# Folding batches 2 to 7 of a Fourier stage with accumulating transfers

## The chip, the cores and the metric

The kernel runs on one core of one Trainium2 chip. The metric is the device time of one execution in microseconds. Each kernel is run several times, and the median is compared. The profile is that of one further execution, with its own time and its own span (from the first to the last instruction).

## The reference

For each of 8 batches of 3072 x 256 numbers the kernel computes the real part of a two-dimensional Fourier transform, and sends every resulting row through a maxout network: three products with w1, w2 and w3, the largest of the three, and a product with w_out.

```python
def _attn_ref(x):                       # x: (8, 3072, 256) float32
    X = np.fft.fft(x, axis=1)
    X = np.fft.fft(X, axis=2)
    return X.real.astype(np.float32)

def _moe_ref(x, w1, w2, w3, w_out):     # x: (24576, 256), w: (256, 768), w_out: (768, 256)
    h = np.maximum(np.maximum(x @ w1, x @ w2), x @ w3)
    return (h @ w_out).astype(np.float32)
```

## The kernel before

All products run in bf16 on TensorE. The Fourier transform over 256 columns is folded into the weights at the start (`gE`, `gO`, `gD`, `gw`). What is left per batch is the transform over 3072 rows, in two stages, and the network.

**Loading and turning.** The 3072 rows of a batch are split as 24 x 128, the 256 columns as 4 groups of 64. A chunk `xs` has 96 partitions (4 column groups x 24 row groups) and 32 of the 128 rows, with 64 columns each; four chunks make a batch. `load_rows` (L107) and `load_next` (L119) issue the loads on SyncE's queue (SP). Pool then converts each chunk to bf16 and changes the order, so that the 128 rows stand next to each other for each column: the natural half (columns 0 to 32 of a group, L155) and a reversed half (rows and columns backwards, L158). This is `turn_chunk`, cut into four parts per chunk, two natural and two reversed. The real part of the transform combines each value with its mirror image, and the kernel does so inside the matmul.

**Stage one.** `Mix.s` takes the turned tile as stationary operand, one column at a time. For each of 33 columns it runs two matmuls into the same place of PSUM: the natural column against `m24f` (L496) and the reversed column against `m24r` (L498). `m24r` names the mirrored partitions. Pieces s0 to s5 hold five columns each, s6 holds three (0, 32 and 1). ScalarE evicts the piece into `z_all` (L503, L506, L507).

**Stage two.** `Mix.k` runs four matmuls or more per piece against the table `tab` (L522, L524) and ScalarE evicts into `t` (L526). Pieces k0 to k5 each make 256 of the 1536 columns of `t`; `end` adds a last one.

**The network.** A batch has 3 blocks of 512 columns, each with 6 units, one per slice of 128 of the hidden width: 18 units. A unit runs four matmuls of 512 columns (L542, L543), an evicting relu on ScalarE (L556) and a maximum on VectorE (L557), and then two matmuls (L550) that turn the same PSUM banks into the values of the mirrored rows. Twelve times per batch a slot opens a bank `po` (two banks in all) with a matmul (L591); VectorE makes `other` from it (L594), Pool adds that to `even` (L597), twelve hidden matmuls collect in the bank (L567), and VectorE adds bank and `even` into `ot` (L617). Half of `ot` is scattered by Pool (L620, followed by a tiny memset, L624), half is stored by SP (L630). There are six `ot` buffers and two banks `ps` for the pieces and `pl` (L580).

**The order.** Each engine executes its instructions in the order in which the program writes them. The last loop of the program goes over batches, blocks and units, and a plan, `at(b, unit, fn)`, says which further work is written after which unit (units above 17 fall into the next batch). While batch b is in the network, the plan holds the pieces of batch b + 1, from unit `begin[b]` on, one a unit, the turning of batch b + 2 and the loads of batch b + 3:

```python
begin = [11, 6] + [5] * (B - 3)
at(b, 6 + 4 * ch + part if b else 11 + 11 * (4 * ch + part) // 16, ... turn_chunk(b + 2, ch, part))
at(b, UNITS + (0, 1, 2, 4 if b else 6)[ch], lambda b=b, ch=ch: fetch(b + 3, ch))
```

Batch 0 is prepared ahead of the loop and batch 1 mostly in its first units, by code of their own.

Of the kernel before, what the change touches and what calls it, by code (L numbers as in the profile page):

```python
# [10 lines left out]
BF16 = mybir.dt.bfloat16  # L11
INT32 = mybir.dt.int32
AX = mybir.ActivationFunctionType
ALU = mybir.AluOpType
# [19 lines left out]
def kernel(  # L34
# [9 lines left out]
    nc = tc.nc  # L44

    B, S, D = x.shape
# [3 lines left out]
    TOKB = 512  # L50
# [9 lines left out]
    consts = ctx.enter_context(tc.tile_pool(name="consts", bufs=1))  # L60
    ps_f = ctx.enter_context(tc.tile_pool(name="ps_f", bufs=2, space=bass.MemoryType.PSUM))
    xs_pool = ctx.enter_context(tc.tile_pool(name="xs", bufs=4))
    x0_pool = ctx.enter_context(tc.tile_pool(name="x0", bufs=2))
    t_pool = ctx.enter_context(tc.tile_pool(name="tbuf", bufs=2))

    m24f = consts.tile([96, 96], BF16, tag="m24f")
# [28 lines left out]
    t_mid = consts.tile([128, 2, B], BF16, tag="t_mid")  # L95
    z_all = consts.tile([128, 128 * 26], BF16, tag="z_all")
    z = z_all.rearrange("p (c r) -> p c r", r=26)

    def x_rows(b):
        return x[b].rearrange("(a bb) (g dl) -> g a bb dl", bb=128, g=4)  # L100
# [31 lines left out]
    raw = {}  # L132
    turned = {}

    def reverse(copy, xr, xs, r0, n, d0=32, d1=65):

        last = r0 + n > 128
        for (lo, hi, m) in ((d0, min(d1, 64), n), (64, d1, n - 1)) if last else ((d0, d1, n),):
            if lo < hi:
                copy(out=xr[:, lo - 32:hi - 32, 129 - r0 - m:129 - r0],  # L140
                     in_=bass.AP(xs.tensor, xs.offset + (m - 1) * 64 + lo,
                                 [xs.ap[0], [1, hi - lo], [-64, m]]))

    def turn_chunk(b, ch, part=None):

        if (b, "v") not in turned:
            x0 = x0_pool.tile([96, 66 * 130], BF16, name="x0", tag="x0")
            v = x0.rearrange("p (dl bb) -> p dl bb", bb=130)
            turned[b] = (lambda d: v[:, d, 0:128], rows_back(v[:, 33:66, :]))
            turned[b, "v"] = v  # L150
        v = turned[b, "v"]
        xs = raw[b, ch]
        for (d0, d1) in (((0, 17), (17, 33))[part % 2:part % 2 + 1] if part is not None else ((0, 33),)):
            if part is None or part < 2:
                nc.gpsimd.tensor_copy(v[:, d0:d1, ch * 32:ch * 32 + 32],  # L155
                                      xs[:, 0:32 * 64].rearrange("p (bb dl) -> p dl bb", dl=64)[:, d0:d1, :])
            if part is None or part >= 2:
                reverse(lambda out, in_: nc.gpsimd.tensor_copy(out, in_), v[:, 33:66, :], xs,  # L158
                        ch * 32, 33 if ch == 3 else 32, 32 + d0, 32 + d1)

    def signed():
        nc.scalar.activation(out=gw[:, 514:770], in_=gw[:, 256:512], func=AX.Copy, scale=sgn)
# [17 lines left out]
    def rows_back(v):  # L180
        return lambda d: v[:, 32 - d, 0:128] if d else v[:, 32, 1:129]
# [17 lines left out]
        nc.gpsimd.iota(t, pattern, base=base, channel_multiplier=cm,  # L199
                       allow_small_or_imprecise_dtypes=True)  # L200

    x0_first = x0_pool.tile([96, 64 * 130], BF16, name="x0", tag="x0")
    x0v = x0_first.rearrange("p (bb dl) -> p bb dl", dl=64)
    xs_a = xs_pool.tile([96, 33 * 64], FP32, name="xs", tag="xs")
    rows_a = xs_a.rearrange("p (bb dl) -> p bb dl", dl=64)
    load_rows((nc.sync, nc.sync, nc.scalar, nc.scalar), rows_a[:, 0:16, :], 0, 112, 128)
# [37 lines left out]
    for (name, value) in (("rnd", ROUND), ("n24", -24.0)):  # L244
        c = gen.tile([128, 1], FP32, name=name, tag=name)
# [17 lines left out]
    turn = 2.0 * math.pi  # L263
# [34 lines left out]
    for (r0, r1) in ((0, 3), (3, 7)):  # L298
# [5 lines left out]
                          in_=up[:, 0:13].unsqueeze(1).to_broadcast([96, 2, 13]))  # L304
# [36 lines left out]
    for (m, c, by) in ((m24f, 0, ind24), (m24r, 24, ind24[:, ::-1])):  # L341
        nc.vector.tensor_tensor(
            out=m.rearrange("p (g r) -> p g r", g=4),
            in0=t24[:, c:c + 24].unsqueeze(1).to_broadcast([96, 4, 24]),
            in1=by.unsqueeze(2).to_broadcast([96, 4, 24]), op=ALU.mult)
    for (m, c, own) in ((m0f, 0, 1), (m0r, 24, 3)):
# [7 lines left out]
        out=dvec.rearrange("p (dl g) -> p dl g", g=4),  # L354
# [55 lines left out]
    for ch in range(4):  # L410
# [11 lines left out]
                        in_=moe_w_out.rearrange("(jc p) c -> p jc c", jc=NJC))  # L422
# [56 lines left out]
    class Mix:  # L479
# [7 lines left out]
        def s(self, k, x0, pool=ps_f, evict=nc.scalar.copy):  # L487

            ps1 = pool.tile([128, 512], FP32, name="ps1", tag="ps")
            if k < len(DLS):  # L490
                parts = [(d, 96, m24f, m24r) for d in range(*DLS[k])]
            else:
                parts = [(0, 52, m0f, m0r), (32, 48, m24f, m24r), (1, 96, m24f, m24r)]
            c0 = 0
            for (d, n, mf, mr) in parts:
                nc.tensor.matmul(ps1[:, c0:c0 + n], x0[0](d), mf[:, 0:n],  # L496
                                 start=True, stop=False)
                nc.tensor.matmul(ps1[:, c0:c0 + n], x0[1](d), mr[:, 0:n],  # L498
                                 start=False, stop=True)
                c0 += n  # L500
            if k < len(DLS):
                lo = 4 * DLS[k][0]
                evict(out=z[:, lo:lo + 20, 0:24],  # L503
                      in_=ps1[:, 0:480].rearrange("p (c r) -> p c r", r=24))
            else:
                evict(out=z_all[:, 0:52], in_=ps1[:, 0:52])  # L506
                evict(out=z[:, 2:8, 0:24],  # L507
                      in_=ps1[:, 52:196].rearrange("p (c r) -> p c r", r=24))
# [42 lines left out]
                             skip_group_check=True)  # L551

    def unit_out(pses, dst, n):
        stmp = h_pool.tile([128, TOKB], BF16, name="stmp", tag="stmp")
        src3 = pses[1][:, 0:n]
        nc.scalar.activation(out=stmp[:, 0:n], in_=pses[0][:, 0:n], func=AX.Relu)  # L556
        nc.vector.tensor_tensor(out=dst, in0=src3, in1=stmp[:, 0:n], op=ALU.max)  # L557
# [6 lines left out]
    def l2_hidden(po, hcols):  # L564
        for jc in range(NJC):
            yield
            nc.tensor.matmul(po, hcols(jc), wout_bf[:, jc * 256:(jc + 1) * 256],  # L567
                             start=False, stop=(jc == NJC - 1), skip_group_check=True)
# [101 lines left out]
    def l2_mid():  # L670

        hmid = h_pool.tile([128, NJC, B], BF16, name="hmid", tag="hmid")
        n = NJC * B
        psm = ps_f.tile([128, 512], FP32, name="psm", tag="ps")
        for i in range(2):
            for jc in range(NJC):
                js = slice(jc * 128, (jc + 1) * 128)
                cs = slice(i * n + jc * B, i * n + (jc + 1) * B)
                nc.tensor.matmul(psm[:, cs], gE[i][:, js], t_mid[:, 0, :],
                                 start=True, stop=False)  # L680
                nc.tensor.matmul(psm[:, cs], gO[i][:, js], t_mid[:, 1, :],
                                 start=False, stop=True)
                yield
        stmp = h_pool.tile([128, TOKB], BF16, name="stmp", tag="stmp")
        nc.scalar.activation(out=stmp[:, 0:n], in_=psm[:, 0:n], func=AX.Relu)
        nc.vector.tensor_tensor(out=hmid.rearrange("p jc n -> p (jc n)"), in0=psm[:, n:2 * n],
                                in1=stmp[:, 0:n], op=ALU.max)
        po = ps_f.tile([128, 512], FP32, name="pom", tag="ps")
        for _ in range(6):
            yield  # L690
        for k in range(2):
            nc.tensor.matmul(po[0:B, 0:256], t_mid[:, k, :], gw[:, k * 256:(k + 1) * 256],
                             start=(k == 0), stop=(k == 1))
            yield
        yield from l2_hidden(po[0:B, 0:256], lambda jc: hmid[:, jc, :])
        ot = out_pool.tile([128, 512], FP32, name="ot", tag="ot")
        nc.vector.tensor_copy(out=ot[0:B, 0:256], in_=po[0:B, 0:256])
        stored(nc.sync.dma_start(out=out[NHALF: NHALF + S * (B - 1) + 1: S, :],
                                 in_=ot[0:B, 0:256]), "direct", ("scattered",))
# [28 lines left out]
    first = prep_first(0, lambda: slots.pop(0).tile([128, 512], FP32, name="psg", tag="ps"))  # L728
# [10 lines left out]
    h_pool = ctx.enter_context(tc.tile_pool(name="hbuf", bufs=2))  # L739
# [23 lines left out]
    def at(b, unit, fn):  # L763
        plan.setdefault((b + unit // UNITS, unit % UNITS), []).append(fn)

    def piece(b, what):
        mm = mix(b)
        if what[0] == "s":
            mm.s(int(what[1:]), turned[b])
        elif what[0] == "k":  # L770
            mm.k(int(what[1]))
        else:
            mm.end()
# [4 lines left out]
    ahead = (("s0",), ("s1",), ("s2",), ("s3",), ("s4",), ("s5",), ("s6",),  # L778
             ("k0",), ("k1",), ("k2",), ("k3",), ("k4",), ("k5", "end"))
    first_ahead = (11, 12, 13, 13, 14, 14, 15, 16, 16, 17, 18, 19, 20)  # L780
    begin = [11, 6] + [5] * (B - 3)

    def l2_first():
        for _ in l2_even(0, 0):
# [17 lines left out]
    for b in range(B - 1):  # L802
        for i, whats in enumerate(ahead):
            for what in whats:
                at(b, begin[b] + i if b else first_ahead[i], lambda b=b, what=what: piece(b + 1, what))
        if b + 2 < B:
            for ch in range(4):
                for part in range(4):
                    at(b, 6 + 4 * ch + part if b else 11 + 11 * (4 * ch + part) // 16,
                       lambda b=b, ch=ch, part=part: turn_chunk(b + 2, ch, part))  # L810
                if b + 3 < B:
                    at(b, UNITS + (0, 1, 2, 4 if b else 6)[ch], lambda b=b, ch=ch: fetch(b + 3, ch))

    for b in range(B):
# [77 lines left out]
```

## Time and profile before

| | us |
|---|---|
| median of 3 runs | 413.03 |
| lowest and highest of them | 412.92, 413.54 |
| the profiled execution | 412.64 |
| its span | 410.9 |
| TensorE busy | 397.4 |
| Pool busy | 320.7 |
| VectorE busy | 308.7 |
| ScalarE busy | 266.5 |

In the profile's rows PE is TensorE's matmuls, PEld its loads of the stationary operand, DVE VectorE, ACT ScalarE, POOL GpSimd and SP SyncE; a q behind the name is that engine's queue of issued instructions. A row names the line of the program, the operation, the tile written and the tiles read, shapes and count. The idle time given with a group is the time that the engine stood still just before its instructions, and the arrow names what ended it. Rows of a timeline begin with start and length in microseconds from the start of the span. The ends of matmuls are modelled, so their starts are the better measure.

### The profile page before, as it was taken

Reading aid. Unit: us, or ns where it says so; the run is one execution under the profiler, and the core shown is the slowest. Engines: PE = TensorE matmul, PEld = TensorE weight load, DVE = VectorE, ACT = ScalarE, POOL = GpSimd, SP = SyncE. Lnnn points to the kernel's source line nnn. Section 1 sums busy time; section 2 is a strip of 40 time slices with the busy share of each in tenths; the row PEclk is TensorE's granted clock in tenths of the full one; section 3 lists DMA queues with packets and bytes.
Section 4 is the critical chain, followed back from the end, with each engine's and each line's share of the span. In section 5 each row is a group of like instructions: output and inputs, shape, how many; then the busy total and the mean of one; then the engine's idle time right before and its main releaser. Section 6 shows DMA issues by size and latency. Waiting matters only on the chain.

```text
span 410.9 us, 9097 instructions
## 1 busy us (share of the span) xinstructions
PE 397.4 (97%) x3072; PEld 269.2 (66%) x3072; DVE 308.7 (75%) x556; ACT 266.5 (65%) x489; POOL 320.7 (78%) x428
## 2 busy tenths in 40 slices
PE   0999999999999999999999999999999999999996
PEld 0465677766676677667666667667666666766665
DVE  8798767776768777786778777787768767778884
ACT  6787766766666667657765766666775676655550
POOL 9599999998888888888789798888878844446651
PEclk9999999999999999999999999999999999999999
DMA  9999885784228841586218942386411121212214
GB/s 116 185 198 183 188 210 143 184 193 104 100 80 210 181 130 53 144 209 139 99 65 191 193 133 86 95 195 144 143 65 70 61 78 64 79 53 53 104 65 142
DMA packets 131111, 52.70 MB, mean 128 GB/s; under 512 B 113009, under 2 KB 128120, under 8 KB 131064
## 3 DMA queue, kind: packets, MB, share of 16 engines
q1 hardware_dynamic: 106496, 37.50, 37.5%
q0 software_dynamic: 23632, 14.29, 16.3%
q8 instruction: 24, 0.39, 0.4%
q10 hardware_dynamic: 936, 0.33, 0.3%
q14 instruction: 23, 0.19, 0.2%
HBM read 29.02 MB, written 25.17 MB: 132 GB/s over the span
## 4 chain that ended last, share of the span: by engine, by line
PE 95%; DVE 2%; ACT 1%; issue 0%; POOL 0%; ACTq 0%; POOLq 0%
PE po L567 30%; PE pse L542 15%; PE pse L550 15%; PE pse L543 15%; PE ps L496 3%; PE ps L498 3%; PE po L591 3%; PE ps L522 3%; PE ps L524 3%; PE pl L580 2%; PE warm L713 2%; DVE hm L557 1%; PE psw L465 0%; DVE w L276 0%; ACT stmp L556 0%
## 5 line engine op out<-in xcount | busy, mean ns | idle before, releaser
L556 ACT ACTIVATE stmp<-pse 128x512 bf16<-128x512 f32 x288 | 171.2, 600 | 44.7 <-PE pse L543 29.7
L557 DVE TENSOR_TENSOR hp<-pse,stmp 128x512 bf16<-128x512 f32 x144 | 99.6, 691 | 87.2 <-ACT stmp L556 60.1
L620 POOL DMA_INDIRECT out_dram<-ot,rows_m x92 | 102.8, 1118 | 53.2 <-DVE ot L617 40.1
L542 PE MATMUL pse<-t,gE 128*128 128x512 bf16 x288 | 109.2, 379 | 0.5
L543 PE MATMUL pse<-t,gO 128*128 128x512 bf16 x288 | 109.0, 378 | 0.0
L557 DVE TENSOR_TENSOR hm<-pse,stmp 128x512 bf16<-128x512 f32 x144 | 99.2, 689 | 3.8 <-ACT stmp L556 3.5
L567 PE MATMUL po<-wout_bf,hp 128*128 128x256 bf16 x576 | 85.9, 272 | 0.0
L550 PE MATMUL pse<-t,gD 128*128 128x512 bf16 x288 | 85.6, 379 | 0.0
L567 PE MATMUL po<-wout_bf,hm 128*128 128x256 bf16 x570 | 85.3, 273 | 0.0
L597 POOL TENSOR_TENSOR even<-even,other 128x256 f32<-128x256 f32 x92 | 66.5, 723 | 22.3 <-DVE other L594 19.8
L567 PEld LDWEIGHTS <-hp 128*128 128x128 bf16 x576 | 56.3, 98 | 17.1 <-issue 1.9
L567 PEld LDWEIGHTS <-hm 128*128 128x128 bf16 x576 | 56.4, 98 | 16.6
L617 DVE TENSOR_TENSOR ot<-po,even 128x512 f32<-128x512 f32 x92 | 62.8, 682 | 0.0
L158 POOL CAST x<-xs 96x544 bf16<-96x544 f32 (+5 forms) x57 | 60.7, 1071 | 0.0
L155 POOL CAST x<-xs 96x544 bf16<-96x544 f32 (+2 forms) x51 | 59.0, 1159 | 0.3 <-DMA xs<-in_x_dram 0.3
L526 ACT CAST t<-ps 128x512 bf16<-128x512 f32 x48 | 27.9, 586 | 34.5 <-PE ps L524 34.4
L550 PEld LDWEIGHTS <-gD 128*128 128x128 bf16 x288 | 27.9, 98 | 32.2
L503 ACT CAST z_all<-ps 128x480 bf16<-128x480 f32 x46 | 25.4, 560 | 33.7 <-PE ps L498 33.7
L594 DVE SCALAR_TENSOR_TENSOR other<-twice,po 128x256 f32<-128x256 f32 x92 | 43.8, 476 | 0.1
L543 PEld LDWEIGHTS <-gO 128*128 128x128 bf16 x288 | 28.1, 98 | 20.3 <-issue 2.0
L542 PEld LDWEIGHTS <-gE 128*128 128x128 bf16 x288 | 28.1, 98 | 19.6 <-issue 0.7
L583 ACT COPY even<-pl 128x512 f32<-128x512 f32 x46 | 27.0, 588 | 10.1 <-PE pl L580 10.1
(171 smaller groups left out, 383.7 us busy)
## 6 DMA issues: line engine op xcount, KB each, us to landing
xs<-in_x_dram SPq DMA_DIRECT2D x84, 198.0 KB
out_dram<-ot SPq DMA_DIRECT2D x90, 128.0 KB
xs<-in_x_dram SPq DMA_DIRECT2D x28, 192.0 KB
raw_w<-in_moe_w_dram SPq DMA_DIRECT2D x4, 384.0 KB
out_dram<-ot,rows_m POOLq DMA_INDIRECT x92, 3.8
out_dram<-ot SPq DMA_DIRECT2D x17, 64.0 KB
x<-in_x_dram POOLq DMA_DIRECT2D x8, 120.0 KB, 6.1
xs<-in_x_dram SPq DMA_DIRECT2D x32, 5.8 KB
```

Source lines behind the costliest of these rows:

```text
L155: nc.gpsimd.tensor_copy(v[:, d0:d1, ch * 32:ch * 32 + 32], xs[:, 0:32 * 64].rearrange("p (bb dl) -> p dl bb", dl=64)[:, d0:d1, :])
L158: reverse(lambda out, in_: nc.gpsimd.tensor_copy(out, in_), v[:, 33:66, :], xs, ch * 32, 33 if ch == 3 else 32, 32 + d0, 32 + d1)
L542: nc.tensor.matmul(pse[:, 0:n], gE[i][:, js], te, start=True, stop=False)
L543: nc.tensor.matmul(pse[:, 0:n], gO[i][:, js], to, start=False, stop=True)
L550: nc.tensor.matmul(pse, gD[i][:, js], to, start=False, stop=True, skip_group_check=True)
L556: nc.scalar.activation(out=stmp[:, 0:n], in_=pses[0][:, 0:n], func=AX.Relu)
L557: nc.vector.tensor_tensor(out=dst, in0=src3, in1=stmp[:, 0:n], op=ALU.max)
L567: nc.tensor.matmul(po, hcols(jc), wout_bf[:, jc * 256:(jc + 1) * 256], start=False, stop=(jc == NJC - 1), skip_group_check=True)
L594: nc.vector.scalar_tensor_tensor(out=other, in0=twice, scalar=po[:, 256:257], in1=po[:, 0:256], op0=ALU.mult, op1=ALU.subtract)
L597: nc.gpsimd.tensor_tensor(out=line[:, 256:512], in0=line[:, 0:256], in1=other, op=ALU.add)
L617: nc.vector.tensor_tensor(out=ot, in0=po, in1=lin, op=ALU.add)
L620: stored(nc.gpsimd.indirect_dma_start(out, bass.IndirectOffsetOnAxis(ap=rows_m[0:128 - lo, b * 12 + slot: b * 12 + slot + 1], axis=0), ot[ ...
```

## The change

For batches 2 to 7 the sum of each value and its mirror image is formed before stage one. Pool writes the natural half into a tile `xw` and the mirrored half, with rows and columns backwards, into one buffer `xb`; column 33 of `xw` takes the few values that have no partner. `send_turned` issues eight stores on SP that bring `xb` to DRAM, 12 partitions each. `add_turned` issues two transfers from Pool that read the stored half back with its partitions in reverse order and add it into `xw` (`accum_op`), 16 columns each. `Mix.s` then runs one matmul per column, against `m24f`, and two for column 0 alone.

The plan moves with it. In batches from 1 on, the parts of the turning stand at units 5 to 18 instead of 6 to 21, in an order that brings the mirrored parts of the last two chunks ahead of their natural parts; the sends stand at unit 16 and the adds at unit 20 (in batch 0 at 20 and 24). The pieces begin at unit 9 in batch 1 and at unit 6 in the later ones, one later than before, and in batch 6 none stands later than unit 17. The pitch of the turned tile goes from 130 to 128, the tile of batches 0 and 1 has one buffer, and `stmp` is 16 columns wider. Batches 0 and 1 keep their two matmuls per column.

```diff
@@ -60,7 +60,9 @@
     consts = ctx.enter_context(tc.tile_pool(name="consts", bufs=1))
     ps_f = ctx.enter_context(tc.tile_pool(name="ps_f", bufs=2, space=bass.MemoryType.PSUM))
     xs_pool = ctx.enter_context(tc.tile_pool(name="xs", bufs=4))
-    x0_pool = ctx.enter_context(tc.tile_pool(name="x0", bufs=2))
+    x0_pool = ctx.enter_context(tc.tile_pool(name="x0", bufs=1))
+    xw_pool = ctx.enter_context(tc.tile_pool(name="xw", bufs=2))
+    turn_pool = ctx.enter_context(tc.tile_pool(name="turn", bufs=2, space=bass.MemoryType.DRAM))
     t_pool = ctx.enter_context(tc.tile_pool(name="tbuf", bufs=2))
 
     m24f = consts.tile([96, 96], BF16, tag="m24f")
@@ -95,6 +97,8 @@
     t_mid = consts.tile([128, 2, B], BF16, tag="t_mid")
     z_all = consts.tile([128, 128 * 26], BF16, tag="z_all")
     z = z_all.rearrange("p (c r) -> p c r", r=26)
+    xb = consts.tile([96, 32 * 128], BF16, tag="xb")
+    mir = xb.rearrange("p (dl bb) -> p dl bb", bb=128)
 
     def x_rows(b):
         return x[b].rearrange("(a bb) (g dl) -> g a bb dl", bb=128, g=4)
@@ -141,22 +145,61 @@
                      in_=bass.AP(xs.tensor, xs.offset + (m - 1) * 64 + lo,
                                  [xs.ap[0], [1, hi - lo], [-64, m]]))
 
-    def turn_chunk(b, ch, part=None):
+    def turn_chunk(b, ch):
 
         if (b, "v") not in turned:
-            x0 = x0_pool.tile([96, 66 * 130], BF16, name="x0", tag="x0")
-            v = x0.rearrange("p (dl bb) -> p dl bb", bb=130)
+            x0 = x0_pool.tile([96, 68 * 128], BF16, name="x0", tag="x0")
+            v = x0[:, 0:66 * 130].rearrange("p (dl bb) -> p dl bb", bb=130)
             turned[b] = (lambda d: v[:, d, 0:128], rows_back(v[:, 33:66, :]))
             turned[b, "v"] = v
         v = turned[b, "v"]
         xs = raw[b, ch]
-        for (d0, d1) in (((0, 17), (17, 33))[part % 2:part % 2 + 1] if part is not None else ((0, 33),)):
-            if part is None or part < 2:
-                nc.gpsimd.tensor_copy(v[:, d0:d1, ch * 32:ch * 32 + 32],
-                                      xs[:, 0:32 * 64].rearrange("p (bb dl) -> p dl bb", dl=64)[:, d0:d1, :])
-            if part is None or part >= 2:
-                reverse(lambda out, in_: nc.gpsimd.tensor_copy(out, in_), v[:, 33:66, :], xs,
-                        ch * 32, 33 if ch == 3 else 32, 32 + d0, 32 + d1)
+        nc.gpsimd.tensor_copy(v[:, 0:33, ch * 32:ch * 32 + 32],
+                              xs[:, 0:32 * 64].rearrange("p (bb dl) -> p dl bb", dl=64)[:, 0:33, :])
+        reverse(lambda out, in_: nc.gpsimd.tensor_copy(out, in_), v[:, 33:66, :], xs,
+                ch * 32, 33 if ch == 3 else 32)
+
+    def turn_part(b, ch, part):
+
+        xs = raw[b, ch]
+        if b not in turned:
+            xw = xw_pool.tile([96, 34 * 128], BF16, name="xw", tag="xw")
+            turned[b] = xw.rearrange("p (dl bb) -> p dl bb", bb=128)
+        v = turned[b]
+        half, natural = part % 2, part // 2
+        if natural:
+            d0, d1 = ((0, 17), (17, 33))[half]
+            nc.gpsimd.tensor_copy(v[:, d0:d1, ch * 32:ch * 32 + 32],
+                                  xs[:, 0:32 * 64].rearrange("p (bb dl) -> p dl bb", dl=64)[:, d0:d1, :])
+            return
+        c0 = 96 - 32 * ch
+        d0, d1 = ((0, 16), (16, 32))[half]
+        nc.gpsimd.tensor_copy(mir[:, d0:d1, c0:c0 + 32],
+                              bass.AP(xs.tensor, xs.offset + 33 * 64 - 1 - d0,
+                                      [xs.ap[0], [-1, d1 - d0], [-64, 32]]))
+        if half:
+            nc.gpsimd.tensor_copy(v[:, 33, c0:c0 + 32],
+                                  bass.AP(xs.tensor, xs.offset + 32 * 64, [xs.ap[0], [-64, 32]]))
+
+    held = {}
+
+    def send_turned(b):
+
+        hd = turn_pool.tile([8, 12 * 4096], BF16, name="held", tag="held")
+        for i in range(8):
+            nc.sync.dma_start(out=hd[7 - i].rearrange("(a r) -> a r", a=12),
+                              in_=xb[i * 12:(i + 1) * 12])
+        held[b] = hd
+
+    def add_turned(b):
+
+        hd = held[b]
+        v = turned[b]
+        for c in range(2):
+            nc.gpsimd.dma_start(out=v[:, 1 + 16 * c:17 + 16 * c, :].rearrange("p dl bb -> p (dl bb)"),
+                                in_=bass.AP(hd.tensor, hd.offset + 11 * 4096 + 2048 * c,
+                                            [[12 * 4096, 8], [-4096, 12], [1, 2048]]),
+                                accum_op=ALU.add)
 
     def signed():
         nc.scalar.activation(out=gw[:, 514:770], in_=gw[:, 256:512], func=AX.Copy, scale=sgn)
@@ -199,8 +242,8 @@
         nc.gpsimd.iota(t, pattern, base=base, channel_multiplier=cm,
                        allow_small_or_imprecise_dtypes=True)
 
-    x0_first = x0_pool.tile([96, 64 * 130], BF16, name="x0", tag="x0")
-    x0v = x0_first.rearrange("p (bb dl) -> p bb dl", dl=64)
+    x0_first = x0_pool.tile([96, 68 * 128], BF16, name="x0", tag="x0")
+    x0v = x0_first[:, 0:64 * 128].rearrange("p (bb dl) -> p bb dl", dl=64)
     xs_a = xs_pool.tile([96, 33 * 64], FP32, name="xs", tag="xs")
     rows_a = xs_a.rearrange("p (bb dl) -> p bb dl", dl=64)
     load_rows((nc.sync, nc.sync, nc.scalar, nc.scalar), rows_a[:, 0:16, :], 0, 112, 128)
@@ -493,10 +536,15 @@
                 parts = [(0, 52, m0f, m0r), (32, 48, m24f, m24r), (1, 96, m24f, m24r)]
             c0 = 0
             for (d, n, mf, mr) in parts:
-                nc.tensor.matmul(ps1[:, c0:c0 + n], x0[0](d), mf[:, 0:n],
-                                 start=True, stop=False)
-                nc.tensor.matmul(ps1[:, c0:c0 + n], x0[1](d), mr[:, 0:n],
-                                 start=False, stop=True)
+                if isinstance(x0, tuple):
+                    pairs = ((x0[0](d), mf), (x0[1](d), mr))
+                elif d:
+                    pairs = ((x0[:, d, :], mf),)
+                else:
+                    pairs = ((x0[:, 0, :], mf), (x0[:, 33, :], mr))
+                for i, (st, mv) in enumerate(pairs):
+                    nc.tensor.matmul(ps1[:, c0:c0 + n], st, mv[:, 0:n], start=(i == 0),
+                                     stop=(i == len(pairs) - 1))
                 c0 += n
             if k < len(DLS):
                 lo = 4 * DLS[k][0]
@@ -551,7 +599,7 @@
                              skip_group_check=True)
 
     def unit_out(pses, dst, n):
-        stmp = h_pool.tile([128, TOKB], BF16, name="stmp", tag="stmp")
+        stmp = h_pool.tile([128, TOKB + 16], BF16, name="stmp", tag="stmp")
         src3 = pses[1][:, 0:n]
         nc.scalar.activation(out=stmp[:, 0:n], in_=pses[0][:, 0:n], func=AX.Relu)
         nc.vector.tensor_tensor(out=dst, in0=src3, in1=stmp[:, 0:n], op=ALU.max)
@@ -681,7 +729,7 @@
                 nc.tensor.matmul(psm[:, cs], gO[i][:, js], t_mid[:, 1, :],
                                  start=False, stop=True)
                 yield
-        stmp = h_pool.tile([128, TOKB], BF16, name="stmp", tag="stmp")
+        stmp = h_pool.tile([128, TOKB + 16], BF16, name="stmp", tag="stmp")
         nc.scalar.activation(out=stmp[:, 0:n], in_=psm[:, 0:n], func=AX.Relu)
         nc.vector.tensor_tensor(out=hmid.rearrange("p jc n -> p (jc n)"), in0=psm[:, n:2 * n],
                                 in1=stmp[:, 0:n], op=ALU.max)
@@ -778,7 +826,9 @@
     ahead = (("s0",), ("s1",), ("s2",), ("s3",), ("s4",), ("s5",), ("s6",),
              ("k0",), ("k1",), ("k2",), ("k3",), ("k4",), ("k5", "end"))
     first_ahead = (11, 12, 13, 13, 14, 14, 15, 16, 16, 17, 18, 19, 20)
-    begin = [11, 6] + [5] * (B - 3)
+    begin = [11, 9] + [6] * (B - 3)
+    turn_order = [(ch, part) for ch, part in zip((0, 0, 0, 0, 1, 1, 1, 1, 2, 2, 3, 3, 2, 2, 3, 3),
+                                                 (0, 1, 2, 3, 0, 1, 2, 3, 0, 1, 0, 1, 2, 3, 2, 3))]
 
     def l2_first():
         for _ in l2_even(0, 0):
@@ -802,13 +852,16 @@
     for b in range(B - 1):
         for i, whats in enumerate(ahead):
             for what in whats:
-                at(b, begin[b] + i if b else first_ahead[i], lambda b=b, what=what: piece(b + 1, what))
+                at(b, min(begin[b] + i, 17 if b == B - 2 else 99) if b else first_ahead[i],
+                   lambda b=b, what=what: piece(b + 1, what))
         if b + 2 < B:
-            for ch in range(4):
-                for part in range(4):
-                    at(b, 6 + 4 * ch + part if b else 11 + 11 * (4 * ch + part) // 16,
-                       lambda b=b, ch=ch, part=part: turn_chunk(b + 2, ch, part))
-                if b + 3 < B:
+            first, width, send_at, add_at = (5, 14, 16, 20) if b else (11, 11, 20, 24)
+            for i, (ch, part) in enumerate(turn_order):
+                at(b, first + width * i // 16, lambda b=b, ch=ch, part=part: turn_part(b + 2, ch, part))
+            at(b, send_at, lambda b=b: send_turned(b + 2))
+            at(b, add_at, lambda b=b: add_turned(b + 2))
+            if b + 3 < B:
+                for ch in range(4):
                     at(b, UNITS + (0, 1, 2, 4 if b else 6)[ch], lambda b=b, ch=ch: fetch(b + 3, ch))
 
     for b in range(B):
```

## The prediction

> **What bounds the kernel now.** I read the page's busy times and granted clock first, then the chain of work that ended last.
>
> ```profile
> PE 397.4 (97%) x3072; PEld 269.2 (66%) x3072; DVE 308.7 (75%) x556; ACT 266.5 (65%) x489; POOL 320.7 (78%) x428
> ...
> PEclk9999999999999999999999999999999999999999
> ...
> PE 95%; DVE 2%; ACT 1%; issue 0%; POOL 0%; ACTq 0%; POOLq 0%
> ```
>
> TensorE is busy for 97% of the span at the full granted clock, and 95% of the chain runs through it. A busy share alone proves little, since the ends of matmuls are modelled; what counts is the pitch at which they start. The timeline of TensorE shows it for one stage-one piece and its neighbours (start, length, line, tile):
>
> ```profile
> 181.18 0.21 PE L496 MATMUL ps<-m24f,x 96*128 96x96 bf16 x1
> 181.22 0.20 PE L498 MATMUL ps<-m24r,x 96*128 96x96 bf16 x1
> ...
> 181.56 0.21 PE L498 MATMUL ps<-m24r,x 96*128 96x96 bf16 x1
> 181.60 0.38 PE L542 MATMUL pse<-t,gE 128*128 128x512 bf16 x1
> ...
> 182.47 0.59 PE L550 MATMUL pse<-t,gD 128*128 128x512 bf16 x2
> 182.90 0.27 PE L591 MATMUL po<-gw,t 128*128 128x257 bf16 x1
> ```
>
> Ten matmuls start within 0.42 us (181.18 to 181.60), 42 ns apart, and the next unit's first matmul starts on the same grid: no wait on either side. The steady rhythm is read from the chain in order of time, where one and the same place comes back each batch:
>
> ```profile
> 168.79 0.98 PE po L567 x9
> ...
> 216.04 0.98 PE po L567 x9
> ...
> 263.40 0.98 PE po L567 x9
> ...
> 310.65 0.98 PE po L567 x9
> ```
>
> A batch takes 47.3 us ((310.65 - 168.79) / 3), a unit (18 per batch) 2.63 us. The next engine is Pool, so I read busy time by stretches (length, then PE, PEld, DVE, ACT, POOL, clock, DMA share, GB/s): one stretch in which the turning of a batch runs, and one late, almost without it.
>
> ```profile
> 204.00:253.00 49.00, 49.00 (x383) 33.66 (x382) 36.41 (x62) 32.16 (x60) 41.60 (x56) 1.00 0.53 135
> ...
> 302.00:351.00 49.00, 49.00 (x387) 34.01 (x386) 37.17 (x63) 31.63 (x59) 32.78 (x47) 1.00 0.20 70
> ```
>
> **The saving on TensorE.** Of the 33 matmul pairs of a batch's stage one (six pieces of 5, one of 3), all but d = 0 become one matmul: 32 go, one of them 48 columns wide. At 42 ns each, the short one at half: 31 x 0.042 + 0.02 = 1.32 us a batch, for batches 2 to 7 7.9 us, all on the engine that sets the end. Nothing is added to TensorE. The batch becomes 46.0 us, the unit 2.55 us.
>
> **Pool.** It issued what the groups of instructions list (count, busy us, mean ns, idle before):
>
> ```profile
> L620 POOL DMA_INDIRECT out_dram<-ot,rows_m x92 | 102.8, 1118 | 53.2 <-DVE ot L617 40.1 <-issue 8.5 <-DMA xs<-in_x_dram 2.3
> L155 POOL CAST x<-xs 96x544 bf16<-96x544 f32 x24 | 27.3, 1137 | 0.0
> L158 POOL CAST x<-xs 96x544 bf16<-96x544 f32 x18 | 20.8, 1155 | 0.0
> L158 POOL CAST x<-xs 96x512 bf16<-96x512 f32 x18 | 19.5, 1086 | 0.0
> L107 POOL DMA_DIRECT2D x<-in_x_dram x12 | 11.8, 1002 | 0.3 <-issue 0.3
> L158 POOL CAST x<-xs 96x561 bf16<-96x561 f32 x6 | 7.0, 1163 | 0.0
> L158 POOL CAST x<-xs 96x495 bf16<-96x495 f32 x6 | 6.3, 1046 | 0.0
> L158 POOL CAST x<-xs 96x32 bf16<-96x32 f32 x6 | 1.4, 228 | 0.0
> ```
>
> The natural casts (L155) stay. The reversed ones cost (20.8 + 19.5 + 7.0 + 6.3 + 1.4) / 6 = 9.2 us a batch; in their place come 8 of 96x512 at 1.086 and 4 of 96x32 at 0.228, 9.6 us: +0.4. Two accumulating DMAs are added. The trace has none; the nearest rows are the plain loads that Pool issues (1.0 us) below and its slowest scatter (2.6 us) above. I take 1.0, since a row of 96 transfers resembles those loads: +2.0. Busy before is 41.6 x 47.3 / 49 = 40.2 us a batch, so 42.6 of 46.0 after, and 44.7 with the 0.17 us (8.5 / 51) of issue gap in front of its 12 scatters: still under TensorE, by 1.3 us. But the 16 casts now fall into 14 units instead of 16, and Pool will run late inside that stretch by 1 to 2 us. Who waits for a late Pool is the final add (L617), through L597:
>
> ```profile
> 182.04 0.72 POOL L597 TENSOR_TENSOR even<-even,other 128x256 f32<-128x256 f32 x1 [0.68 <-DVE other L594]
> ...
> 186.94 0.68 DVE L617 TENSOR_TENSOR ot<-po,even 128x512 f32<-128x512 f32 x1
> ```
>
> The sum ready at 182.76 is used at 186.94: 4.2 us of cover. I price Pool's lag at 0.4 us in all (0 to 3 us); beyond 4.2 us it goes straight to VectorE, then to the two `po` banks and TensorE.
>
> **The new transfers.** One mirrored half is 96 x 4096 x 2 bytes = 0.79 MB. The queue rows and the scatter's landing time:
>
> ```profile
> q1 hardware_dynamic: 106496, 37.50, 37.5%
> q0 software_dynamic: 23632, 14.29, 16.3%
> ...
> DMA to landing us min/median/max: 2.4/3.8/5.7
> ```
>
> q1 spent 0.375 x 16 x 410.9 = 2465 us of engine time on 37.5 MB, 66 us per MB; q0 75. The sends cost 52 us, 3.2 us on 16 engines. An add lies between a plain copy and a copy of both operands: 0.39 MB is 26 to 59 us of engine time, 1.6 to 3.7 us on 16 engines, double on eight. I take both operands on 16 engines. First add: 1.0 issue + 3.8 landing + 3.7 = 8.5 us. It is put at unit 20 and first read by s0 at unit 24, four units or 10.2 us later; the second is read three units later still (17.9 us) and needs 2.0 + 3.8 + 7.4 = 13.2. So batches 3 to 7 do not wait. For batch 2 the add comes at unit 6 of batch 1 and s0 at unit 9, 7.7 us: 0.8 us of wait, between 0 and 6.4 (5.7 landing and eight engines).
>
> The sends go onto SP ahead of the next x loads, which it issues in order:
>
> ```profile
> 40.87 2.31 SPq L119 DMA_DIRECT2D xs<-in_x_dram  x5
> ...
> 203.88 11.70 SPq L630 DMA_DIRECT2D out_dram<-ot  x4
> 215.67 3.16 SPq L107 DMA_DIRECT2D xs<-in_x_dram  x4
> ...
> 235.12 5.77 SPq L119 DMA_DIRECT2D xs<-in_x_dram  x5
> ```
>
> Small transfers took 0.46 us each (2.31 / 5) to 1.15 (5.77 / 5), so eight sends hold SP for 3.7 to 9.2 us; I take 5. Part of that fills time in which SP waited for results (4 stores in 11.7 us). The last x load was issued 25.2 us after the first (240.89 - 215.67); with 4 us of SP delay, 5 of transfers in between and 2 to land it comes at 36. Its first cast, formerly at unit 18 (47 us), is now at unit 13 (33 us): Pool waits some 3 us. That is inside the 4.2 us of cover, so 0, but it takes most of the cover.
>
> **Moved pieces.** Batch 2's pieces start at unit 9, so its second stage-two piece ends batch 1, and batch 2's first unit reads the columns it evicts. The costs:
>
> ```profile
> L526 ACT CAST t<-ps 128x512 bf16<-128x512 f32 x48 | 27.9, 586 | 34.5 <-PE ps L524 34.4
> L556 ACT ACTIVATE stmp<-pse 128x512 bf16<-128x512 f32 x288 | 171.2, 600 | 44.7 <-PE pse L543 29.7
> ```
>
> Between them stand only two L550 matmuls, 0.43 us (182.47 to 182.90). The eviction takes 0.59, perhaps behind a 0.60 activation: 0.2 to 0.8 us of wait, I take 0.6. In batch 6 the last three pieces share unit 17 and want three of the two `ps` banks: 0.3 us (0 to 0.8), same rows.
>
> **The sum.** 7.9 - 0.4 (Pool) - 0.8 (batch 2's add) - 0.6 - 0.3 = 5.8 us saved. The profiled execution (412.64 us, span 410.9) becomes 406.8; the median of the three runs, 413.03, is 0.39 above it, so the forecast is 407.2. About 0.2% (0.8 us) is what a measurement of this kernel can tell from no change.
>
> **A rule on the transfers.** The Trainium skill, "DMA: Bandwidth & Descriptors", section "Why a DMA increments its semaphore by 16 and not by 1", says a transfer is spread over the largest number of engines up to 16 that divides the slowest dimension of both its sides. The add's source starts with a dimension of 8, so by it the add would run on eight engines. No transfer in this trace shows that case. By that rule the first add would need 12.2 us instead of my 8.5, which is the first rival's case.
>
> **Rivals.** (1) The adds are late (slower). Eight engines, both operands: the first needs 1.0 + 3.8 + 7.4 = 12.2 us, 2.0 too late; the second 2.0 + 3.8 + 14.8 = 20.6, 2.7 too late. That is 2.7 us in each of batches 2 to 6 and 20.6 - 15.4 = 5.2 in batch 1: 18.7 us lost, and 0.9 at the two moved places, against 7.9: 424.7. It decides from where the first transfer takes over 5.4 us. For it: x loads fill the DMA engines in the same units. Against: that phase was never the chain's. Chance 0.14.
>
> (2) Pool becomes the bound. If an add costs Pool 2.6 us, like the slowest scatter, its batch is 44.7 + 3.2 = 47.9 us, 0.6 above today's; over batches 2 to 5 that is +2.4, less batch 6's 1.3: about 414. It decides from 1.65 us each. For it: Pool has the smallest margin. Chance 0.14.
>
> (3) The x loads come later than I think (9.2 us on SP, 7.4 of transfers): 25.2 + 9.2 + 7.4 + 2 = 44 against 33, 11 late, 4.2 covered; even half of the remaining 6.8 us in each of batches 2 to 5 costs 13.6 and gives 413.0 - 5.8 + 13.6 = 420.8. Chance 0.07; a mild form that eats just the gain, 413: 0.05.
>
> **How the numbers follow.** The forecast has 0.60. With no loss the time is 405.1; with its costs at their upper ends short of a rival (3 + 3 + 0.8 + 0.8) it is 412.7. The range goes from 404.9 up to 418, leaving out rival 1's full price and rival 3's. Faster: the forecast and the mild ends of rivals 2 and 3, 0.66; same 0.07; slower 0.27.
>
> **What would show it.** Right: 192 fewer stage-one matmuls at a 42 ns pitch, batches 46.0 us apart, no wait of TensorE ahead of s0 except in batch 1, two Pool DMAs of about 1 us per batch. Wrong: gaps ahead of the pieces released by a DMA on the turned tile; Pool busy without gaps and L617 waiting for L597; Pool casts waiting for x; batches of 47 us or more.

## The result, and the profile after

The changed kernel takes 431.6 us (median of four runs, 426.2 to 433.1) against 413.0 before (four runs): the ratio is 1.041, 95% interval 1.031 to 1.051. It is slower by 4%, where 1.4% faster was forecast. The profiled execution took 431.48 us with a span of 429.7.

The page of the changed kernel (busy times, granted clock, chain) answers to the first lines shown of before:

```profile
PE 392.1 (91%) x2832; PEld 262.1 (61%) x2880; DVE 309.2 (72%) x556; ACT 267.1 (62%) x489; POOL 333.1 (78%) x458
...
PEclk9999999997799999999999989999999999999999
...
PE 57%; DMA 22%; POOL 7%; DVE 4%; issue 4%; ACT 3%; SPq 3%; POOLq 0%; ACTq 0%; DVEq 0%
```

TensorE was 95% of the chain; now transfers hold 22% of it (the adds 13%), and the clock shows places below full. TensorE's timeline names the waits. These are the first pieces (s0) of batches 2, 4, 5, 6 and 7; the bracket is the idle time before them and what ended it:

```profile
105.92 0.56 PE L546 MATMUL ps<-m24f,xw 96*128 96x96 bf16 x5 [8.15 <-DMA xw<-held]
...
198.53 0.37 PE L546 MATMUL ps<-m24f,xw 96*128 96x96 bf16 x5 [3.05 <-DMA xw<-held]
...
247.92 0.37 PE L546 MATMUL ps<-m24f,xw 96*128 96x96 bf16 x5 [3.15 <-DMA xw<-held]
...
297.93 0.37 PE L546 MATMUL ps<-m24f,xw 96*128 96x96 bf16 x5 [2.19 <-DMA xw<-held]
...
345.39 0.37 PE L546 MATMUL ps<-m24f,xw 96*128 96x96 bf16 x5 [0.86 <-DMA xw<-held]
```

With 0.92 us for batch 3 (shown below) that is 18.3 us: in each of the six folded batches TensorE stands in front of s0 until the first add has landed. Pool issued the two adds of each at these times:

```profile
95.68 2.08 POOL L199 DMA_DIRECT2D xw<-held  x2
...
188.61 2.06 POOL L199 DMA_DIRECT2D xw<-held  x2
...
237.80 2.04 POOL L199 DMA_DIRECT2D xw<-held  x2
...
288.88 2.04 POOL L199 DMA_DIRECT2D xw<-held  x2
...
337.67 2.05 POOL L199 DMA_DIRECT2D xw<-held  x2
```

From the start of the issue to s0 it is 10.2, 9.9, 10.1, 9.1 and 7.7 us. TensorE, however, was ready 2.1, 6.9, 7.0, 6.9 and 6.9 us after the issue, not 10.2 (7.7 in batch 1). The window ahead of batch 3's s0 shows where it went (Pool and TensorE in one timeline; the add belongs to unit 20, s0 to unit 24):

```profile
138.28 0.38 PE L590 MATMUL pse<-t,gE 128*128 128x512 bf16 x1
138.71 0.72 POOL L645 TENSOR_TENSOR even<-even,other 128x256 f32<-128x256 f32 x1 [1.31 <-DVE other L642]
139.60 0.98 POOL L668 DMA_INDIRECT out_dram<-ot,rows_m  x1 [0.16 <-DMA xs<-in_x_dram]
140.61 2.04 POOL L199 DMA_DIRECT2D xw<-held  x2
141.25 0.81 PE L590 MATMUL pse<-t,gE 128*128 128x512 bf16 x2
143.52 0.38 PE L590 MATMUL pse<-t,gE 128*128 128x512 bf16 x1
145.80 0.38 PE L590 MATMUL pse<-t,gE 128*128 128x512 bf16 x1
147.93 0.49 PE L615 MATMUL po<-wout_bf,hm 128*128 128x256 bf16 x3
149.34 0.37 PE L546 MATMUL ps<-m24f,xw 96*128 96x96 bf16 x5 [0.92 <-DMA xw<-held]
```

TensorE is through unit 20 at 138.28, but Pool reaches the add only at 140.61, 2.3 us later: ahead of it stand a sum, which waited 1.31 us for VectorE's `other`, and a scatter. And units without a piece can be shorter than 2.55 us (141.25, 143.52 and 145.80 are 2.27 and 2.28 apart). In batches 4 to 7 all four units between add and s0 are empty ones. TensorE needs 9.6 to 9.7 us for them, Pool is 2.8 us late, and 6.9 us are left. In batch 4 the first of these four units begins here, and Pool's add at 188.61:

```profile
185.84 0.38 PE L590 MATMUL pse<-t,gE 128*128 128x512 bf16 x1
```

In batch 1 (the add for batch 2) Pool is later still: TensorE passes unit 6 at 90.6, and the add is issued at 95.68, 5.1 us behind. Between 40.5 and 95.7 us Pool never stands still for more than 0.20 us at a time, so it has no slack there to catch up. The busy tenths of Pool (40 slices of the span) show that phase, nines from the fifth slice to the ninth, first in the kernel before and then in the changed one:

```profile
POOL 9599999998888888888789798888878844446651
```

```profile
POOL 9678999998597799978997879878998764445551
```

A gap also has an after-effect. In the rows of windows (length, PE, PEld, DVE, ACT, POOL, clock, DMA share, GB/s), after the 8.15 us gap, a little later, after the 3.05 us gap and after the 3.15 us gap:

```profile
106.00:112.00 6.00, 5.78 (x26) 3.17 (x27) 1.98 (x3) 2.90 (x5) 1.16 (x3) 0.50 0.58 146
112.00:118.00 6.00, 5.95 (x46) 3.88 (x46) 4.05 (x8) 3.93 (x8) 4.07 (x6) 1.00 0.26 95
198.00:210.00 12.00, 11.37 (x90) 7.64 (x93) 7.83 (x13) 8.77 (x16) 10.29 (x16) 1.00 0.75 151
247.90:260.00 12.10, 11.80 (x85) 7.74 (x88) 7.30 (x13) 7.71 (x14) 9.13 (x13) 0.86 0.65 149
```

For six microseconds TensorE runs at half its clock, with 26 matmuls against 46 in the next six: 3.0 us lost. After 3.15 us of gap it loses 0.14 x 12.1 = 1.7 us, after 3.05 us nothing. The span grew by 18.8 us (410.9 to 429.7); 18.3 us of gaps and 4.7 us of slowed clock, less the 7.9 us that the count saves, give 15.1 of them. The Trainium skill, "TensorE: Matmul & The Clock Gate", section "Part 1: The HAM clock gate (the "warmup" mystery)", gives a free-running activity window of about 3.4 us, after an idle one of which the clock is halved. The half clock agrees; the slowed stretch after 3.15 us of gap shows that here a shorter gap did it too. Nor does the length of the gap alone decide. In e2_sixteen (below) these two gaps stand ahead of a `po`:

```profile
227.34 0.27 PE L639 MATMUL po<-gw,t 128*128 128x257 bf16 x1 [3.07 <-DVE ot L665]
...
276.96 0.27 PE L639 MATMUL po<-gw,t 128*128 128x257 bf16 x1 [1.96 <-DVE ot L665]
```

After the longer one the clock is 1.00 (227.3 to 239.0), after the shorter one 0.56 (277.0 to 280.4).

### The profile page after: what moved, and what is told of

The parts are those of the page before. It is cut to its first block, busy times and chain, and to the rows that moved or that the text cites. A ratio compares the mean times of both kernels' runs of the same rounds, so it can differ in the third digit from the quotient of the medians.

```text
span 429.7 us, 8772 instructions
## 1 busy us (share of the span) xinstructions
PE 392.1 (91%) x2832; PEld 262.1 (61%) x2880; DVE 309.2 (72%) x556; ACT 267.1 (62%) x489; POOL 333.1 (78%) x458
## 3 DMA queue, kind: packets, MB, share of 16 engines
q1 hardware_dynamic: 107648, 42.22, 41.6%
## 4 chain that ended last, share of the span: by engine, by line
PE 57%; DMA 22%; POOL 7%; DVE 4%; issue 4%; ACT 3%; SPq 3%; POOLq 0%; ACTq 0%; DVEq 0%
PE po L615 19%; DMA xw<-held 13%; PE pse L590 10%; PE pse L598 9%; PE pse L591 8%; DMA xs<-in_x_dram 5%; PE ps L546 3%; ACT stmp L604 3%; DMA raw_w<-in_moe_w_dram 2%; PE pl L628 2%; POOL out_dram L668 2%; POOL x L111 2%; DVE hm L605 2%; PE ps L570 2%; PE ps L572 2%
## 5 line engine op out<-in xcount | busy, mean ns | idle before, releaser
L591 PE MATMUL pse<-t,gO 128*128 128x512 bf16 x252 | 96.1, 382 | 0.0
L645 POOL TENSOR_TENSOR even<-even,other 128x256 f32<-128x256 f32 x92 | 70.2, 763 | 25.7 <-DVE other L642 25.6
L598 PE MATMUL pse<-t,gD 128*128 128x512 bf16 x276 | 83.8, 382 | 0.5 <-issue 0.2
L172 POOL CAST xw<-xs 96x544 bf16<-96x544 f32 (+1 forms) x48 | 53.6, 1119 | 0.0
L177 POOL CAST xb<-xs 96x512 bf16<-96x512 f32 x48 | 50.5, 1066 | 0.1
```

Of the source, the lines that this page charges most:

```text
L172: nc.gpsimd.tensor_copy(v[:, d0:d1, ch * 32:ch * 32 + 32], xs[:, 0:32 * 64].rearrange("p (bb dl) -> p dl bb", dl=64)[:, d0:d1, :])
L177: nc.gpsimd.tensor_copy(mir[:, d0:d1, c0:c0 + 32], bass.AP(xs.tensor, xs.offset + 33 * 64 - 1 - d0, [xs.ap[0], [-1, d1 - d0], [-64, 32]]))
L591: nc.tensor.matmul(pse[:, 0:n], gO[i][:, js], to, start=False, stop=True)
L598: nc.tensor.matmul(pse, gD[i][:, js], to, start=False, stop=True, skip_group_check=True)
L645: nc.gpsimd.tensor_tensor(out=line[:, 256:512], in0=line[:, 0:256], in1=other, op=ALU.add)
```

## The experiments

Theory A: the first add lands after TensorE has come to s0, and the waits with the slowed clock are the loss. Theory B: the new work overloads Pool, SP or the DMA engines, wherever the pieces stand.

**The pieces later (e1_later).**

```diff
-    begin = [11, 9] + [6] * (B - 3)
+    steady = tuple(range(8, 21))
+    starts = {0: first_ahead, 1: (13, 13, 14, 14, 15, 15, 16, 16, 17, 18, 19, 20, 21),
+              B - 2: (8, 9, 10, 11, 12, 13, 14, 15, 15, 16, 16, 17, 17)}
...
```

> The stage-one pieces are moved behind the adds: batches 2 to 5 begin at unit 8 instead of 6, batch 6 too, batch 1 at unit 13 instead of 9 with two pieces a unit. Nothing else changes. Theory A (the first add lands after TensorE has reached s0, and the slowed clock after those gaps does the rest): the 18.3 us of waits ahead of s0 fall to under 2 us, the clock stays at 1.00, and the time is 405 to 409 us. Theory B (Pool and the DMA engines are overloaded by the new work, wherever the pieces stand): the waits move to other lines and the time stays above 420 us.

Measured: 413.0 us, ratio to the kernel before 1.001 (0.998 to 1.004). The waits ahead of s0 are gone (0.1 us) and the clock is 1.00, so A holds for 18.6 us of the loss. But the saving is not there either, and the time missed the 405 to 409 us of A, so A is not all. What was left are these waits (waits of TensorE and VectorE: total, times, longest):

```profile
PE po L639 <- DVE ot L665: 5.0, 5, 1.6
...
DVE ot L665 <- DMA out_dram<-ot: 3.7, 3, 1.7
```

TensorE waits for a bank `po`, VectorE for a free `ot`, and that for a store. SP's timeline shows why the store is late:

```profile
235.83 6.16 SPq L111 DMA_DIRECT2D xs<-in_x_dram  x2
242.08 1.14 SPq L678 DMA_DIRECT2D out_dram<-ot  x1
243.32 3.45 SPq L111 DMA_DIRECT2D xs<-in_x_dram  x4
246.81 3.22 SPq L123 DMA_DIRECT2D xs<-in_x_dram  x5
250.14 4.63 SPq L678 DMA_DIRECT2D out_dram<-ot  x8
```

Two x loads alone hold SP for 6.2 us, and afterwards eight stores go out in one burst. In program order seven of them belong to results that VectorE had finished before, the first at 230.0, and stood behind the loads. VectorE waits at the end of it:

```profile
253.23 0.69 DVE L665 TENSOR_TENSOR ot<-po,even 128x512 f32<-128x512 f32 x1 [1.62 <-DMA out_dram<-ot]
```

**No transfers (e4_none).** `send_turned` and `add_turned` are not called, so the kernel leaves out the mirrored half.

> Sends and adds are left out, so the mirrored half is never added; casts, order and the single matmul per column stay. Both theories: no wait ahead of s0, and the saving of 7.9 us on TensorE shows alone: 405 to 407 us. Above 409 would mean that the casts, the moved pieces or the new layout cost something by themselves.

Measured: 406.5 us, ratio 0.984 (0.981 to 0.988). The fold on TensorE, with casts, layout and moved pieces, is worth 6.1 us by the medians. The sum had 7.9 less 1.3 for these, 6.6.

**The adds into unused space (e5_aside).**

```diff
-            nc.gpsimd.dma_start(out=v[:, 1 + 16 * c:17 + 16 * c, :].rearrange("p dl bb -> p (dl bb)"),
+            nc.gpsimd.dma_start(out=raw_w[c].bitcast(BF16)[0:96, 0:2048],
```

> Sends and adds stay as they are, but the adds go into space that nothing reads (the raw weights' buffers), so the mirrored half is not in the sum and no piece waits for an add. Theory A: what is lost is the wait alone, so 405 to 409 us. Theory B: the load on Pool, SP and the DMA engines is still there, so 415 us or more.

Measured: 411.9 us, ratio 1.000 (0.997 to 1.003). Without any wait for an add the transfers still cost 5.4 us (411.9 - 406.5). That lies between what A and B expected, and both are partly right: some 20 us (431.6 - 411.9) are the waits with the slowed clock, 5 the load. The split is one of the times: the gaps and the slowed clock add up to 23.0 us in the trace, and why 3 us less show in the time is open.

**Only the sends (e9_sends).** `add_turned` is not called.

> The sends stay, the adds are left out, so the mirrored half is not in the sum and no piece waits for a transfer. It splits the 5.4 us between e4_none (406.5) and e5_aside (411.9). If SP is what delays the stores, by eight sends of some 0.5 us a batch, the time stays near 410 to 412. If it is the adds, which take DMA time from the x loads that SP is issuing, it falls to 406.5 to 408.5.

Measured: 406.5 us, ratio 0.984 (0.982 to 0.986): the eight sends cost nothing that can be measured by themselves. The load is that of the adds. Part of its way to TensorE shows in the waits: in e5_aside TensorE waits 3.8 us for `po`, and VectorE 2.3 us for late stores and 0.9 for Pool's sums; in e9_sends no wait for `po` or for a store is left. Whether the adds do this by their time on the DMA engines or by their time on Pool (12 issues of 1.2 us) was not separated.

**Copies instead of adds (e3_plain).** `accum_op` is dropped.

> The transfers into xw are plain copies instead of accumulating ones, so the mirrored half replaces the natural one there; all else as in the changed kernel. If the addition is what makes a transfer of 4096 bytes take 328 ns instead of 159, its landing time falls by about 2 us, from a median of 9.9 us to about 8, and s0 waits some 2 us less per batch: 422 to 427 us. If not, 430.

One execution: 421.05 us, a little below the expected 422 to 427; TensorE's gaps ahead of s0 add up to 12.6 us instead of 18.3. The queue rows of Pool's transfers (packets, MB, share of 16 engines) in the changed kernel, in e3_plain and in e9_sends, which has none of them, with their spans of 429.7, 419.3 and 405.2 us, price one transfer of 4096 bytes:

```profile
q0 software_dynamic: 26128, 19.02, 22.6%
```

```profile
q0 software_dynamic: 26128, 19.01, 20.4%
```

```profile
q0 software_dynamic: 23632, 14.29, 16.0%
```

That is 1554, 1369 and 1037 us of engine time. If the rest of the queue costs in all three what it costs in e9_sends, the 12 x 96 transfers, with the small packets that come with them, take 517 / 1152 = 0.45 us each when they add, 332 / 1152 = 0.29 us when they copy. Pool's issue fell too, from a median of 1.22 us to 0.64 per instruction.

**Sixteen blocks (e2_sixteen).**

```diff
-        hd = turn_pool.tile([8, 12 * 4096], BF16, name="held", tag="held")
-        for i in range(8):
-            nc.sync.dma_start(out=hd[7 - i].rearrange("(a r) -> a r", a=12),
-                              in_=xb[i * 12:(i + 1) * 12])
+        hd = turn_pool.tile([16, 6 * 4096], BF16, name="held", tag="held")
+        for i in range(16):
+            nc.sync.dma_start(out=hd[15 - i].rearrange("(a r) -> a r", a=6),
+                              in_=xb[i * 6:(i + 1) * 6])
...
-                                            [[12 * 4096, 8], [-4096, 12], [1, 2048]]),
+                                            [[6 * 4096, 16], [-4096, 6], [1, 2048]]),
```

> The stored half is laid out in 16 blocks of 6 partitions instead of 8 of 12 (16 sends instead of 8), so the add's source has a first dimension of 16. Theory A with eight engines per add: 96 transfers of 328 ns take 2.0 us on sixteen engines instead of 3.9, the landing time falls from a median of 9.9 us to about 8, and s0 waits about 2 us less in each of batches 2 to 6; but SP issues 8 more sends a batch, 4 to 5 us, which delay the x loads. Time 420 to 427 us. If the number of engines does not matter, the landing time stays at 9 to 10 us and the time at 430 or above.

The landing time of the adds (least, median, most), of the changed kernel and of this one:

```profile
DMA to landing us min/median/max: 7.6/9.9/11.9
```

```profile
DMA to landing us min/median/max: 5.0/8.0/9.9
```

1.9 us less at the median, as expected of eight engines against sixteen. By the section of "DMA: Bandwidth & Descriptors" in the Trainium skill that the prediction cites, the slowest dimension of both sides decides this, and the landing times agree with it (8 blocks against 16 of the source); on which engines the packets ran, no view here shows. The time was missed: 434.9 us, ratio 1.053 (1.049 to 1.057). The waits ahead of s0 fell to 6.2 us, but TensorE's waits for `po` rose to 16.2 us, while VectorE waited 12.2 us for late stores and 7.5 for Pool's sums. Whether the eight more sends on SP or the denser adds delay the stores was not separated.

**The adds one unit earlier (e11_add19).** Unit 19 instead of 20, pieces unmoved.

> The changed kernel with the adds of batches 3 to 7 at unit 19 instead of 20, the pieces where they were. The add is one unit, 2.5 us, earlier in Pool's order, if the sends have landed by then. Theory A (the window between the add's issue and s0 is too short): the waits ahead of s0 in batches 2 to 6, 10.2 us together, fall to 2 us or less, batch 1's 8 us stay, and the time is 418 to 423 us. If Pool stands waiting for the sends instead, the adds are issued no earlier and the time stays near 430.

Measured: 425.5 us, ratio 1.030 (1.026 to 1.034), some 6 us below the changed kernel by the medians. The two intervals overlap (1.031 to 1.051 there), so it is the waits that carry the argument. The group of single matmuls (count, busy, mean ns, idle before and its end) has 9.6 us of waits instead of 18.3:

```profile
L546 PE MATMUL ps<-m24f,xw 96*128 96x96 bf16 x186 | 15.0, 207 | 9.6 <-DMA xw<-held 9.6
```

7.45 of these stand ahead of batch 2's s0, in batch 1, so the five later ones went from 10.2 to 2.1 us, nearly as expected: the window was the matter. The time is above the expected 418 to 423; 4.6 us of waits for `po` came up.

**Eight output buffers (e8_ot8)**, on top of e1_later: `bufs=6` becomes `bufs=8` for `outbuf`.

> The moved pieces of e1_later with eight ot buffers instead of six. In e1_later SP reached the stores of ot late, behind its x loads, and the final add waited for a free ot buffer (3.7 us) and for Pool's sum (2.2 us), then TensorE for the bank po (5.0 us). Theory C (what is left after the move is the late stores, through the ot buffers): two more buffers cover 8 us of late stores, the 3.7 us go, TensorE's wait for po falls under 2 us, and the time is 408 to 410.5 us, faster than the kernel before. If Pool's lag is the cause, the wait moves from the stores to the sum and the time stays at 412 to 413.

Measured: 409.5 us, ratio 0.991 (0.989 to 0.994): 0.9% faster than the kernel before, and faster than the changed one. The final add's group in e1_later and in e8_ot8:

```profile
L665 DVE TENSOR_TENSOR ot<-po,even 128x512 f32<-128x512 f32 x92 | 62.7, 682 | 5.9 <-DMA out_dram<-ot 3.7 <-POOL even L645 2.2
```

```profile
L665 DVE TENSOR_TENSOR ot<-po,even 128x512 f32<-128x512 f32 x92 | 62.7, 681 | 2.2 <-POOL even L645 2.2
```

The wait for stores is gone, the one for Pool's sum stays, as theory C has it. Of the 3 us that still lie between this and e9_sends, TensorE's waits for `po` are 1.7; the rest is not explained.

**Batch 2's transfers sooner (e10_sooner)**, on top of e8_ot8: units 19 and 23 instead of 20 and 24.

> e8_ot8 with batch 2's sends and adds one unit earlier in batch 1 (units 1 and 5 instead of 2 and 6), so the sends stand ahead of one more x load on SP. In e8_ot8 Pool could turn batch 3's first chunk only when the sends had left the one buffer, and TensorE waited 1.7 us for po at 102 to 105 us. Theory: the sends start some 4 us sooner, that wait goes, and the time falls by 1 to 2 us, to 407.5 to 409. If the later x loads take it back, it stays at 409.5.

Measured: 408.9 us, ratio 0.990 (0.988 to 0.991). That cannot be told from e8_ot8, and a wait of 1.7 us for `po` is still there in the profile, at 98.3 us instead of two at 102 and 105 (1.1 and 0.6). VectorE's final add ahead of it waits 1.72 us for Pool's sum there. The expected cause, the late sends, is thus not shown.

## Why the prediction was wrong

- The saving on TensorE was right: 7.9 us by the count, 6.1 to 6.5 us net in e4_none and e9_sends, where 6.6 net of the small terms was summed. So, nearly, was Pool's issue of an add (1.0 forecast, 1.2 measured): the 2.6 us of rival 2 did not come.
- **The step that failed** is "four units or 10.2 us later ... So batches 3 to 7 do not wait". The unit numbers are places in the program, and the prediction took them for times on Pool as well. Pool came to the add 2.3 us (batch 3) to 2.8 us after TensorE had passed unit 20, since ahead of it stood a scatter and a sum that waited for VectorE, and the empty units in between took 9.6 us, not 10.2. The window was 6.9 to 7.8 us. e11_add19 shows it by moving the add alone: the waits of these batches fell from 10.2 to 2.1 us.
- In batch 1 it put 7.7 us and got 2.1, since Pool was 5.1 us behind. The prediction took Pool's load from a steady stretch (41.6 of 49 us); from 40 to 97 us Pool was already busy for 53.5 of 57 us in the kernel before, and for 54.9 in the changed one. And it priced Pool's lag for the final add alone, not for the place of the transfer in Pool's queue.
- The first add's time was mis-sized less: 8.5 forecast from the start of its issue, 7.7 to 10.2 measured. With the forecast window of 10.2 us none of batches 3 to 7 would have waited.
- The clock after a gap was in no term: about 4.7 us (3.0 + 1.7).
- The x loads: "inside the 4.2 us of cover, so 0". e5_aside and e9_sends show some 5 us for the adds' load. No late cast shows in e5_aside; a part went through the stores of `ot` behind the loads on SP, as e1_later and e8_ot8 show, a place that the prediction did not price.
- Rival 1, the adds late, was the right mechanism at 424.7 us, with a chance of 0.14. Its own rule for the deciding point, a transfer of 5.4 us, rested on the wrong window; by the true window of 6.9 us and its own 4.8 us of issue and landing it decides from 2.1 us, and the forecast's own 3.7 us lay beyond that.
- The moved piece at the end of batch 1 cost 0.24 us, 0.6 was forecast.

What stays open is the adds' load: the late stores explain a part of the 5 us, and no run moved the adds to a time at which Pool or the DMA engines had room.

## What to carry to other kernels

A place in a written-out order is a time only on the engine that sets the pace; for a transfer issued by another engine, look up in the trace when that engine came to its instructions at that place, and count what it waits for there. Compare the window with the landing time in the shortest units, not the mean ones. And when a transfer is added to a phase whose loads fill the DMA engines, look at what else the issuing queue of those loads has to send: here two more output buffers and pieces moved back by two units (four in batch 1) turned a loss of 4% into a gain of 1%. Last, look whether the engine that issues has slack in that phase; a steady stretch need not stand for the start.

## What was not expected of the hardware

A transfer of 4096 bytes that adds took about 0.45 us of engine time against 0.29 for a copy. An add with a source of 8 blocks landed 1.9 us later at the median than one of 16. After a gap of 8.15 us TensorE ran at half its clock for some 6 us, and one of 3.15 us lowered it to 0.86 over the next 12 us, while one of 3.05 us did not; in e2_sixteen one of 1.96 us was followed by 0.56 over 3.4 us and one of 3.07 us by the full clock.
